# A gated mix of a long convolution and an MLP: sorting the filter with GpSimd before its transposes

## The chip, the cores and the metric

The kernel runs on one core of one Trainium2 chip. The metric is the time of one launch on the device in microseconds (us); lower is better. The engines are named as in the profile: PE is TensorE (PEld its weight loads), DVE is VectorE, ACT is ScalarE, POOL is GpSimd, and SP is SyncE, which here only issues transfers.

## The reference

Two branches read the same input `x = A_q` (2048 rows of 640) and are mixed by one gate per row. Cut to what matters:

```python
x = A_q
g = sigmoid((x * gate_w).sum(-1, keepdims=True))

# branch A: a short filter on k (4 taps), times v, then a long filter over the rows, per column
k_shift = sum(k_pad[:, t:t + S, :] * shift_k[:, ks - 1 - t] for t in range(4))
kv = k_shift * v
y = irfft(rfft(pad(kv)) * rfft(pad(ssm_k)))[:S] + kv * ssm_D
a = q * y

# branch B: an MLP over shifted groups of columns, and a second MLP
h = gelu(layernorm(x) @ w1)
x1 = x + shifted(h) @ w2
b = x1 + gelu(layernorm(x1) @ w3) @ w4

out = g * a + (1 - g) * b
```

`A_ssm_k`, the long filter, is given with columns along the first axis: 640 by 2048. The convolution needs it as rows by columns, like `kv`.

## The kernel before

The 2048 rows lie on 128 partitions with 16 rows each (`NT = 16`); the 640 columns are five chunks of 128 (`DC = 5`). The convolution is a Fourier transform made of matrix products with tables of sines: `step1` transforms the rows of `KV` (the product of the short filter and v) and of `HT0` (the long filter), writes the result to a scratch tensor in memory (`S_x`, `S_h`), `gather` reads it back in another order, `step2` makes the second stage, `product` multiplies the two spectra, `step3`, `S_g`, `gin` and `step4` go back. Beside it run `mlp1`, `w2` (first MLP) and `w3`, `w4` (second MLP).

Nothing is scheduled by the compiler: the text `ORDER` is one long list of steps, such as `step1.KV.3.VAVAVAAAAA:2` (second part of a call with its arguments), and `emit` runs through it. Each engine executes its own instructions in that order. Letters in a name say which engine empties a PSUM tile: `A` for ACT, `V` for DVE (`evac`, L323 to L327). A planner wrote the list; only the list is in the kernel.

What the change touches:

- `load_h` brings one chunk of the long filter (128 columns by 2048 rows, 512 KB) into SBUF. Chunks 0 to 2 share a large tile `E`; chunks 3 and 4 take a buffer `HN` of a ring of four (tag `gt`). The same ring later holds index tables (`n`, `ab`), a row of gate sums (`zr`), a tile of ones and the MLP's `gt` tiles. Whoever takes a buffer of the ring waits until its former owner has been read.
- `h_transpose` (L340 to L358) turns a chunk for `HT0`. Partition p of the wanted layout holds even rows in its lower half and odd rows in its upper half, so each step of 16 is turned by two transposes of 64 columns of weights each, one for each half of the array (L352): 32 per chunk, 160 in all. ACT or DVE then empties PSUM into `HT0`.
- `kv_consts` (L500) makes `DG`, 20 diagonal matrices of the short filter's taps, by one DVE multiplication of the identity with the taps (L503). `tap` (L543) uses them: it multiplies transposed chunks of k (`KT`) with these diagonals on PE, and DVE multiplies with v in place (L554 or L557).
- `x_stats`, `rstd_of` (L610, L611), `x_norm` (L617), `x_turn`: statistics of four rows of x, their reciprocal roots on POOL, the normed rows `xn`, and their transposition, for groups 0 and 1 on PE and for 2 and 3 by a transposing DMA (L605).
- `z_rows` (L674 on PE, four ACT copies to `zr` at L679, four small DMAs to `Zs` at L682) and `z_cols` make the sums for the gate.
- `v_load` issues an indirect DMA on POOL's queue (L150) behind whatever POOL was given before.
- `h_shift` copies shifted parts of the MLP's hidden layer into `HM` on DVE (L719, L700, L703).

The half transposes and the rule of the ring, as the code has them:

```python
for r in range(2):
    PE.transpose(out=ps[HALF[r], i, :], in_=hv[:, 8 * hh + i, r, :], identity=IDB[:], tile_position=(0, H * r))
hn = ring.tile([P, S], BF16, name="HN", tag="gt", bufs=GTB)
```

Of the kernel before, what the change touches and what calls it, by code (L numbers as in the profile page):

```python
# [10 lines left out]
ALU = mybir.AluOpType  # L11
BF16 = mybir.dt.bfloat16
# [4 lines left out]
P = 128  # L17
# [3 lines left out]
NT = 16  # L21
H = 64
NG = 32
DC = 5
# [17 lines left out]
def kernel(  # L42
# [23 lines left out]
    GTB = 4  # L66
# [272 lines left out]

    def h_transpose(dc, ev):  # L340
        if "HT0" not in st:
            st["HT0"] = main.tile([P, NT * D], BF16, name="HT0", tag="RT")
        hv = st.pop(("HN", dc)).rearrange("p (t2 r t1) -> p t1 r t2", r=2, t1=NT)
        dst = st["HT0"][:].rearrange("p (t d) -> p t d", t=NT)
        def make(hh):
            box = {}

            def first():
                ps = box["ps"] = psc.tile([P, 8, P], BF16, name="pst", tag="c")
                for i in range(8):  # L350
                    for r in range(2):
                        PE.transpose(out=ps[HALF[r], i, :], in_=hv[:, 8 * hh + i, r, :], identity=IDB[:], tile_position=(0, H * r))  # L352

            def second():
                evac(ev[hh], dst[:, 8 * hh:8 * hh + 8, dc * P:(dc + 1) * P], box["ps"][:])
            return first, second

        return banks(2, make)  # L358
# [141 lines left out]
    def kv_consts():  # L500

        st["DG"] = pool("A2").tile([P, DC * 4, P], BF16, name="DG")
        V.tensor_tensor(out=st["DG"][:], in0=IDB[:].unsqueeze(1).to_broadcast([P, DC * 4, P]),  # L503
                        in1=st["cr"][:].rearrange("p k j -> p (k j)").unsqueeze(2).to_broadcast([P, DC * 4, P]), op=ALU.mult)
# [310 lines left out]
    def step4(t1, ev):  # L815
# [32 lines left out]
        "open.L1.left:0 open.A2.right:0 kv_alloc:0 warm:0 load_x0.0:0 consts0:0 load_x0.1:0 k_load.3.AAA:0 load_cj:0 "  # L848
        "consts0:1 f4_table:0 f1_table:0 k_load.1.AAV:0 k_load.2.AAA:0 f4_table:1 f1_table:1 load_x.1:0 k_load.0.AAA:0 "
        "x_stats.0.VVVA:0 x_stats.0.VVVA:1 x_stats.0.VVVA:2 x_stats.0.VVVA:3 x_stats.0.VVVA:4 row_order:0 load_w1:0 "  # L850
        "k_load.3.AAA:5 load_gw:0 k_load.3.AAA:6 k_load.3.AAA:3 k_load.3.AAA:1 k_load.1.AAV:1 k_load.1.AAV:5 "
        "x_stats.0.VVVA:5 k_load.3.AAA:4 k_load.1.AAV:3 load_x.3:0 k_load.3.AAA:2 k_load.1.AAV:2 kv_consts:0 "
        "k_load.2.AAA:3 v_load.3:0 k_load.1.AAV:4 x_stats.0.VVVA:6 x_norm.0.VVVV:0 x_norm.0.VVVV:1 x_norm.0.VVVV:2 "
        "k_load.1.AAV:6 k_load.2.AAA:1 k_load.2.AAA:4 k_load.2.AAA:2 d_fold:0 x_turn.0.VAV:0 x_norm.0.VVVV:3 "
        "x_turn.0.VAV:4 v_load.2:0 k_load.2.AAA:5 x_turn.0.VAV:1 x_turn.0.VAV:2 k_load.2.AAA:6 x_turn.0.VAV:3 "
        "x_turn.0.VAV:5 tap.7.AA:0 tap.7.AA:1 k_load.0.AAA:1 k_wrap:0 tap.9.VA:0 x_stats.1.VVVV:0 x_stats.1.VVVV:1 "
        "x_stats.1.VVVV:2 x_stats.1.VVVV:3 tap.9.VA:1 tap.7.AA:3 k_load.0.AAA:2 load_h.0:0 tap.7.AA:4 x_stats.1.VVVV:4 "
        "k_load.0.AAA:5 tap.9.VA:3 mlp1.0.1:0 tap.5.AV:0 v_load.1:0 x_stats.1.VVVV:5 tap.9.VA:2 k_load.0.AAA:6 "
        "load_x.2:0 tap.7.AA:2 tap.5.AV:3 tap.5.AV:4 mlp1.0.1:1 w1_mixed:0 tap.5.AV:1 tap.6.VA:0 tap.6.VA:1 tap.6.VA:2 "
        "tap.8.VA:0 k_load.0.AAA:3 tap.5.AV:2 mlp1.0.0:0 load_h.1:0 x_norm.1.VVVV:0 x_norm.1.VVVV:1 x_norm.1.VVVV:2 "  # L860
        "x_norm.1.VVVV:3 x_stats.3.VVAA:0 x_stats.3.VVAA:1 tap.6.VA:3 v_load.0:0 tap.8.VA:1 x_stats.3.VVAA:2 "
        "x_turn.1.AAV:4 tap.8.VA:3 x_stats.3.VVAA:3 k_load.0.AAA:4 x_turn.1.AAV:2 x_turn.1.AAV:5 x_turn.1.AAV:0 "
        "x_stats.3.VVAA:4 mlp1.0.2:0 x_stats.3.VVAA:5 x_stats.3.VVAA:6 tap.8.VA:4 x_stats.3.VVAA:7 x_turn.1.AAV:3 "
        "tap.8.VA:2 tap.4.AV:0 tap.6.VA:4 x_turn.1.AAV:1 mlp1.0.0:1 tap.4.AV:1 tap.9.VA:4 x_norm.3.VVVV:0 tap.4.AV:3 "
        "x_norm.3.VVVV:1 tap.4.AV:4 x_norm.3.VVVV:2 tap.3.AA:0 mlp1.0.2:1 x_norm.3.VVVV:3 tap.3.AA:1 mlp1.1.1:0 "
        "tap.3.AA:3 step1.KV.3.VAVAVAAAAA:0 x_stats.2.VVAA:0 step1.KV.3.VAVAVAAAAA:1 step1.KV.3.VAVAVAAAAA:6 "
        "x_stats.2.VVAA:1 x_stats.2.VVAA:2 x_stats.2.VVAA:3 step1.KV.3.VAVAVAAAAA:2 step1.KV.3.VAVAVAAAAA:7 mlp1.1.0:0 "
        "tap.3.AA:4 step1.KV.3.VAVAVAAAAA:8 x_stats.2.VVAA:4 x_stats.2.VVAA:5 tap.0.VV:0 x_stats.2.VVAA:6 x_turn.3.D:0 "
        "tap.4.AV:2 tap.0.VV:3 tap.0.VV:1 mlp1.1.0:1 load_h.3:0 tap.2.AA:0 mlp1.1.1:1 x_stats.2.VVAA:7 tap.0.VV:4 "
        "mlp1.1.2:0 tap.0.VV:2 x_norm.2.VVVA:0 tap.2.AA:3 step1.KV.3.VAVAVAAAAA:3 x_norm.2.VVVA:1 x_norm.2.VVVA:2 "  # L870
        "tap.2.AA:1 step1.KV.3.VAVAVAAAAA:4 x_norm.2.VVVA:3 h_shift.0:0 step1.KV.3.VAVAVAAAAA:5 "
        "step1.KV.3.VAVAVAAAAA:9 step1.KV.3.VAVAVAAAAA:11 mlp1.1.2:1 mlp1.3.0:0 t2_table:0 step1.KV.3.VAVAVAAAAA:10 "
        "tap.2.AA:4 step1.KV.3.VAVAVAAAAA:12 step1.KV.3.VAVAVAAAAA:13 h_shift.0:1 mlp1.3.0:1 tap.1.VV:0 mlp1.3.2:0 "
        "tap.1.VV:1 h_shift.0:2 x_turn.2.D:0 step1.KV.3.VAVAVAAAAA:14 tap.2.AA:2 step1.KV.3.VAVAVAAAAA:16 mlp1.3.1:0 "
        "step1.KV.2.VAAVVAAVAV:6 tap.1.VV:3 tap.1.VV:2 mlp1.3.2:1 step1.KV.2.VAAVVAAVAV:8 tap.1.VV:4 "
        "step1.KV.3.VAVAVAAAAA:15 tap.3.AA:2 step1.KV.2.VAAVVAAVAV:3 step1.KV.2.VAAVVAAVAV:4 t2_table:1 mlp1.2.1:0 "
        "step1.KV.2.VAAVVAAVAV:5 step1.KV.2.VAAVVAAVAV:7 step1.KV.1.AVVAVVAAVA:9 mlp1.3.1:1 step1.KV.1.AVVAVVAAVA:11 "
        "h_shift.1:0 step1.KV.1.AVVAVVAAVA:6 h_shift.0:3 step1.KV.1.AVVAVVAAVA:8 mlp1.2.2:0 step1.KV.1.AVVAVVAAVA:10 "
        "mlp1.2.1:1 load_w2:0 step1.KV.1.AVVAVVAAVA:0 step1.KV.1.AVVAVVAAVA:1 load_h.2:0 h_shift.3:0 h_shift.3:1 "
        "step1.KV.1.AVVAVVAAVA:7 z_rows:0 h_shift.1:1 step1.KV.1.AVVAVVAAVA:12 step1.KV.1.AVVAVVAAVA:2 mlp1.2.0:0 "  # L880
        "mlp1.2.2:1 z_rows:1 step1.KV.1.AVVAVVAAVA:14 step1.KV.1.AVVAVVAAVA:13 step1.KV.1.AVVAVVAAVA:3 "
        "step1.KV.1.AVVAVVAAVA:5 h_shift.3:2 z_rows:2 h_shift.2:0 step1.KV.2.VAAVVAAVAV:9 h_shift.1:2 "
        "step1.KV.1.AVVAVVAAVA:4 step1.KV.2.VAAVVAAVAV:10 w2.0:0 h_shift.2:1 step1.KV.2.VAAVVAAVAV:11 "
        "step1.KV.2.VAAVVAAVAV:0 w2.0:1 mlp1.2.0:1 step1.KV.2.VAAVVAAVAV:12 step1.KV.2.VAAVVAAVAV:13 "
        "step1.KV.2.VAAVVAAVAV:1 h_shift.2:2 w2.15:0 h_transpose.0.VV:2 h_shift.1:3 h_transpose.2.AV:2 "
        "step1.KV.2.VAAVVAAVAV:2 t2_table:2 h_transpose.1.VA:2 step1.KV.2.VAAVVAAVAV:14 h_transpose.0.VV:3 "
        "h_transpose.2.AV:3 w2.15:1 h_transpose.1.VA:0 h_transpose.2.AV:0 h_transpose.2.AV:1 h_transpose.1.VA:1 "
        "h_transpose.0.VV:0 w2.2:0 step1.KV.0.AAAAVAAAAA:0 step1.KV.1.AVVAVVAAVA:16 h_transpose.1.VA:3 "
        "step1.KV.1.AVVAVVAAVA:15 h_transpose.0.VV:1 step1.KV.0.AAAAVAAAAA:1 step1.KV.0.AAAAVAAAAA:6 h_shift.3:3 "
        "load_h.4:0 step1.KV.0.AAAAVAAAAA:8 w2.2:1 step1.KV.0.AAAAVAAAAA:7 step1.KV.0.AAAAVAAAAA:2 w2.12:0 "  # L890
        "step1.KV.0.AAAAVAAAAA:12 w2.2:2 step1.KV.2.VAAVVAAVAV:15 step1.KV.0.AAAAVAAAAA:9 step1.KV.0.AAAAVAAAAA:10 "
        "t2_table:3 t2_table:4 step1.KV.0.AAAAVAAAAA:11 w2.1:0 w2.12:1 step1.KV.0.AAAAVAAAAA:13 "
        "step1.KV.0.AAAAVAAAAA:14 step1.KV.0.AAAAVAAAAA:3 h_shift.2:3 step1.KV.0.AAAAVAAAAA:5 step1.KV.2.VAAVVAAVAV:16 "
        "step1.KV.0.AAAAVAAAAA:4 h_transpose.4.AV:0 h_transpose.4.AV:2 h_transpose.4.AV:3 h_transpose.3.AV:0 "
        "h_transpose.4.AV:1 h_transpose.3.AV:2 z_cols:0 load_w3:0 w2.1:1 h_transpose.3.AV:3 h_transpose.3.AV:1 "
        "step1.KV.0.AAAAVAAAAA:16 step1.KV.0.AAAAVAAAAA:15 z_cols:1 w2.0:2 z_cols:2 w2.3:0 i_tables:0 "
        "step1.HT0.2.AAVAAAAVAA:6 step1.HT0.2.AAVAAAAVAA:8 step1.HT0.2.AAVAAAAVAA:3 step1.HT0.2.AAVAAAAVAA:5 "
        "step1.HT0.2.AAVAAAAVAA:4 z_cols:3 w2.3:1 step1.HT0.2.AAVAAAAVAA:7 w2.10:0 w2.10:1 w2.1:2 swap.A2.C.right:0 "
# [156 lines left out]
```

## Time and profile before

| what | value |
|---|---|
| median of 3 runs | 241.06 us (240.78 to 244.64) |
| the profiled execution | 242.35 us, of which the span of instructions is 240.6 us |
| mean granted clock of PE in it | 0.984 |
| busy: PE, DVE, ACT, POOL | 227.9, 193.3, 170.4, 19.1 us |
| transposes of the long filter (L352) | 160 matmuls, 5.6 us (from `E`) and 3.8 us (from `HN`) of PE busy time |
| the diagonals (L503, DVE) | 1 instruction, 2.83 us, begun at 8.73 us |
| bytes moved by DMA | 57.08 MB, mean 237 GB/s |

The page of a profile gives each engine's busy time, then the span in 40 slices of 6 us with a digit for tenths of busy time, then the chain of work that ended last: for each instruction what released it, back to the start. A group of instructions is a line of code, an engine, an operation and shapes, with its count, its total busy time and the mean of one in ns. Matmuls overlap each other on PE, so the mean of one is longer than the step from one to the next; the step is read from the chain. Times inside the span are counted from its start.

### The profile page before, as it was taken

The page shows a single profiled execution, that of the slowest core. Times are in us where ns is not written, and L with a number is a line of the kernel's source. Part 1 is how long each engine was busy: PE and PEld are TensorE (multiplying, and loading weights), DVE is VectorE, ACT ScalarE, POOL GpSimd, SP SyncE. Part 2 cuts the span into 40 slices and gives each one's busy share as a digit, 9 for nine tenths or more (in the row PEclk, how much of TensorE's full clock was granted, in tenths as well). Part 3 has the DMA queues.
Part 4 walks back from the last instruction along what each step waited for, and adds up shares of the span by engine and source line. Part 5 has one row for each costly group of instructions (what it writes and reads, how often), then busy time and mean ns, then how long its engine had stood idle before and what let it go on. Part 6 is the DMA issues. An engine that isn't in the chain of part 4 may idle for free.

```text
span 240.6 us, 5764 instructions
## 1 busy us (share of the span) xinstructions
PE 227.9 (95%) x2328; PEld 117.7 (49%) x2328; DVE 193.3 (80%) x449; ACT 170.4 (71%) x303; POOL 19.1 (8%) x32
## 2 busy tenths in 40 slices
PE   6598999999999999999999999999999999989991
PEld 2585755433858445344355334444444345446660
DVE  7876999988876999756679999867688999209994
ACT  4689999779587899899577677675598533436530
POOL 3540322000000020002200300000000000000000
PEclk9689999999999999999999999999999999999999
DMA  6999608693989889994989936199830127689674
GB/s 218 389 379 417 224 2 198 163 343 121 348 302 344 207 346 277 374 385 170 291 206 271 207 121 223 34 244 392 318 110 3 48 107 259 214 301 347 147 276 165
DMA packets 42744, 57.08 MB, mean 237 GB/s; under 512 B 20313, under 2 KB 35418, under 8 KB 42462
## 3 DMA queue, kind: packets, MB, share of 16 engines
q1 hardware_dynamic: 42142, 54.10, 68.5%
q0 software_dynamic: 576, 2.62, 2.9%
q8 instruction: 18, 0.29, 0.5%
q14 instruction: 8, 0.07, 0.1%
HBM read 34.42 MB, written 18.36 MB: 219 GB/s over the span
## 4 chain that ended last, share of the span: by engine, by line
PE 74%; DMA 13%; DVE 9%; POOL 2%; issue 1%; SPq 0%; DVEq 0%
PE ps L788 20%; PE ps L806 15%; PE psw L740 10%; PE psm L663 8%; PE ps L378 5%; PE ps L417 4%; DMA KV<-in_A_v_dram,ROWS 4%; PE pst L352 4%; PE ps L464 3%; PE psk L543 3%; DMA ax<-S_h 2%; DMA q<-in_A_q_dram 2%; DMA gin<-S_g 2%; DVE X L843 2%; DVE q L839 2%; POOL RS L610 2%
## 5 line engine op out<-in xcount | busy, mean ns | idle before, releaser
L806 PE MATMUL ps<-W,gt 128*128 128x512 bf16 (+1 forms) x384 | 56.6, 300 | 0.0
L788 PE MATMUL ps<-x1t,W 128*128 128x512 bf16 x240 | 55.6, 380 | 0.0
L806 PEld LDWEIGHTS <-gt 128*128 128x128 bf16 x384 | 29.0, 98 | 24.9 <-issue 4.6
L788 PEld LDWEIGHTS <-W 128*128 128x128 bf16 x240 | 21.8, 98 | 29.2 <-issue 5.6
L325 ACT CAST stg<-ps 128x512 bf16<-128x512 f32 x51 | 27.3, 597 | 6.7 <-PE ps L378 5.8
L793 ACT ACTIVATE gt<-ps 128x1024 bf16<-128x1024 f32 x24 | 24.8, 1031 | 6.4 <-PE ps L788 6.1
L325 ACT CAST gs<-ps 128x320 bf16<-128x320 f32 x36 | 13.9, 431 | 16.7 <-PE ps L464 11.7
L663 PE MATMUL psm<-xt,WA 128*128 128x512 bf16 x100 | 23.5, 380 | 0.0
L740 PE MATMUL psw<-WA,HT 128*128 128x512 bf16 (+1 forms) x116 | 21.5, 300 | 0.0
L327 DVE CAST stg<-ps 128x512 bf16<-128x512 f32 x29 | 19.3, 683 | 2.5 <-PE ps L378 1.9
L325 ACT CAST hs<-ps 128x512 bf16<-128x512 f32 x28 | 15.2, 591 | 8.3 <-PE ps L417 8.2
L327 DVE CAST gs<-ps 128x320 bf16<-128x320 f32 x28 | 12.7, 485 | 5.6 <-PE ps L464 3.8
L833 ACT ACTIVATE y<-ps,GS 128x320 bf16<-128x320 f32 x19 | 9.7, 526 | 10.0 <-PE ps L829 8.5
L327 DVE CAST XS<-ps 128x512 bf16<-128x512 f32 x18 | 11.8, 684 | 5.7 <-PE ps L417 5.7
L808 DVE SCALAR_TENSOR_TENSOR X<-ps,OMG,X 128x640 bf16<-128x640 f32 x16 | 14.0, 877 | 1.7 <-PE ps L806 1.7
L839 DVE SCALAR_TENSOR_TENSOR q<-ps,GS,q 128x320 bf16<-128x320 f32 x13 | 7.1, 546 | 9.7 <-PE ps L829 9.7
L325 ACT CAST XS<-ps 128x512 bf16<-128x512 f32 x22 | 11.9, 593 | 4.0 <-PE ps L417 3.7
L740 PEld LDWEIGHTS <-HT 128*128 128x128 bf16 x116 | 9.3, 98 | 11.2 <-issue 3.0
L663 PEld LDWEIGHTS <-WA 128*128 128x128 bf16 x100 | 9.0, 98 | 11.5 <-issue 1.6
L742 DVE SCALAR_TENSOR_TENSOR X<-psw,X 128x640 bf16<-128x640 f32 x16 | 12.9, 818 | 0.9 <-PE psw L740 0.7
L417 PE MATMUL ps<-ax,CMP 64*32 64x512 bf16 (+3 forms) x512 | 13.0, 300 | 0.5 <-DMA ax<-S_h 0.5
L745 ACT ACTIVATE jk<-X 128x640 bf16<-128x640 bf16 x16 | 12.0, 751 | 0.0
(141 smaller groups left out, 356.0 us busy)
## 6 DMA issues: line engine op xcount, KB each, us to landing
S_x<-stg SPq DMA_DIRECT2D x8, 640.0 KB
ax<-S_x SPq DMA_DIRECT2D x8, 640.0 KB
S_h<-stg SPq DMA_DIRECT2D x8, 640.0 KB
ax<-S_h SPq DMA_DIRECT2D x8, 640.0 KB
S_g<-gs SPq DMA_DIRECT2D x8, 640.0 KB
W<-in_B_w_dram SPq DMA_DIRECT2D x2, 1920.0 KB
kn<-in_A_k_dram SPq DMA_DIRECT2D x4, 640.0 KB
q<-in_A_q_dram SPq DMA_DIRECT2D x4, 640.0 KB
```

What stands on the lines that cost most here:

```text
L325: A.copy(out=dst, in_=src)
L327: V.tensor_copy(out=dst, in_=src)
L378: PE.matmul(ps[r][:], lhsT=F1[HALF[r]].rearrange("p a b -> p (a b)"), rhs=src[HALF[r], o + 512 * u:o + 512 * u + 512], start=True, stop=Tr ...
L417: PE.matmul(ps[j][q:q + 32, lo - 512 * u:hi - 512 * u], lhsT=CMP[HALF[j], 8 * b + 4 * h + i, c, :], rhs=st[name, 2 * b + h][HALF[j], i, lo ...
L663: PE.matmul(ps[:, v, :].rearrange("p (a b) -> p a b", a=4), lhsT=W1N[:, k, 160 * f:160 * f + P] if f < 4 else W1M[:, k, :], rhs=xt[:, :, k ...
L740: PE.matmul(ps[:, o:o + w], lhsT=h_tile(f, t1), rhs=W2P[:, f, o:o + w], start=(f == 0), stop=(f == 4))
L742: V.scalar_tensor_tensor(out=X1[:, t1, :], in0=ps[:], scalar=1.0, in1=X[:, t1, :], op0=ALU.mult, op1=ALU.add, accum_out=S12[:, 0, t1:t1 + 1])
L745: A.activation(out=jk[:], in_=X1[:, t1, :], func=ACT.Square, accum_out=S12[:, 1, t1:t1 + 1])
L788: PE.matmul(ps[:, u, :].rearrange("p (a b) -> p a b", a=4), lhsT=st["W3"][:, k, f * P:(f + 1) * P], rhs=xt[:, :, k, :], start=(k == 0), st ...
L793: A.activation(out=gt[:, 2 * (fp % 2):2 * (fp % 2) + 2, :], in_=ps[:], func=ACT.Gelu_apprx_tanh)
L806: PE.matmul(ps[:, o:o + w], lhsT=st["gt", c, f // 4][:, f % 4, i * P:(i + 1) * P], rhs=st["W4"][:, f, o:o + w], start=(f == 0), stop=(f == ...
L808: V.scalar_tensor_tensor(out=X1[:, t1, :], in0=ps[:], scalar=OMG[:, t1:t1 + 1], in1=X1[:, t1, :], op0=ALU.mult, op1=ALU.add)
```

## The change

Three things change, and with them the whole list.

1. A new step `h_sort` lets POOL copy each loaded chunk of the filter into a new tile `HP` (a buffer of the ring `gt`), sorted so that the 64 even and 64 odd rows of a step lie behind one another. It reads every 32nd element of two bytes and writes densely. `h_transpose` then turns 128 by 128 elements at once: 16 per chunk, 80 in all.
2. `DG` is made by one POOL select from the taps, spread over the diagonal, instead of DVE's multiplication.
3. `ORDER` is written anew (the letters too), with five `h_sort` steps in it.

```diff
+    def h_sort(dc):
+        hp = ring.tile([P, NT, 2, H], BF16, name="HP", tag="gt", bufs=GTB)
+        G.tensor_copy(out=hp[:], in_=st.pop(("HN", dc)).rearrange("p (q r t) -> p t r q", r=2, t=NT))
+        st["HP", dc] = hp[:].rearrange("p t r q -> p t (r q)")
+
     def h_transpose(dc, ev):
...
-        hv = st.pop(("HN", dc)).rearrange("p (t2 r t1) -> p t1 r t2", r=2, t1=NT)
+        hv = st.pop(("HP", dc))
...
-                    for r in range(2):
-                        PE.transpose(out=ps[HALF[r], i, :], in_=hv[:, 8 * hh + i, r, :], identity=IDB[:], tile_position=(0, H * r))
+                    PE.transpose(out=ps[:, i, :], in_=hv[:, 8 * hh + i, :], identity=IDB[:])
...
-        V.tensor_tensor(out=st["DG"][:], in0=IDB[:].unsqueeze(1).to_broadcast([P, DC * 4, P]),
-                        in1=st["cr"][:].rearrange("p k j -> p (k j)").unsqueeze(2).to_broadcast([P, DC * 4, P]), op=ALU.mult)
+        G.affine_select(out=st["DG"][:], in_=st["cr"][:].rearrange("p k j -> p (k j)").unsqueeze(2).to_broadcast([P, DC * 4, P]), compare_op=ALU.is_equal, fill=0.0,
+                        base=0, pattern=[[0, DC * 4], [-1, P]], channel_multiplier=1)
```

Of the new list, the part that the prediction speaks of most, around the five sorts (cut):

```diff
+        "... step1.KV.3.VAAVAAVAAA:4 tap.0.AV:3 tap.0.AV:1 tap.0.AV:4 h_sort.4:0 x_turn.2.D:0 tap.4.AV:0 tap.4.AV:3 "
+        "tap.4.AV:4 h_sort.3:0 step1.KV.3.VAAVAAVAAA:15 ... tap.0.AV:2 z_rows:0 step1.KV.2.AAVAVAAAAV:4 "
+        "step1.KV.3.VAAVAAVAAA:16 mlp1.3.2:1 tap.1.VA:3 z_rows:1 ... z_rows:2 ... "
+        "step1.KV.1.VAAVVAVAVA:6 h_sort.1:0 ... h_transpose.3.AA:0 h_shift.1:2 h_transpose.4.VV:0 ... "
+        "h_transpose.1.VA:2 ... h_transpose.1.VA:0 ... h_sort.2:0 w2.3:0 ... w2.15:0 ... h_sort.0:0 ... w2.2:0 ... "
+        "h_transpose.2.AV:2 ... h_transpose.2.AV:0 h_transpose.2.AV:1 h_transpose.0.VV:0 ..."
```

On POOL's own queue the order becomes: the constants, the ones of `z_cols`, the row numbers, two v loads (chunks 3 and 2), the roots of `x_stats.0`, the select for `DG`, the v load of chunk 0, the roots of `x_stats.1`, the v load of chunk 1, the roots of `x_stats.3` and of `x_stats.2`, the five sorts (chunks 4, 3, 1, 2, 0), then the four roots of `x1_norm`. Before, the first v load stood ahead of the first roots and the next two behind them. The waits that the new list gives to the sorts: the sort of chunk 4 waits for its load and for an early table on ACT; that of chunk 3 for its load and for the sort of chunk 4; that of chunk 1 for the four small DMAs of `z_rows` (its buffer held `zr`); that of chunk 2 for the last transpose of chunk 1; that of chunk 0 for the last transpose of chunk 4. The copies to `zr` on ACT wait for the sort of chunk 3.

## The prediction

> **What bounds the kernel now.** I read the page's busy times and slices first.
>
> ```profile
> PE 227.9 (95%) x2328; PEld 117.7 (49%) x2328; DVE 193.3 (80%) x449; ACT 170.4 (71%) x303; POOL 19.1 (8%) x32
> PE   6598999999999999999999999999999999989991
> DVE  7876999988876999756679999867688999209994
> POOL 3540322000000020002200300000000000000000
> ```
>
> PE is full from the fourth slice to the tail; POOL all but idle after the seventh. Whether full means bound is read in the chain that ended last, in order of time (start, length, what):
>
> ```profile
> 12.90 10.10 DMA KV<-in_A_v_dram,ROWS
> 23.13 0.42 DVE KV L554
> 23.70 0.60 DVE KV L557
> 24.35 1.99 PE psk L543 x38
> ...
> 61.66 5.50 PE pst L352 x96
> ...
> 72.95 3.71 PE pst L352 x64
> ...
> 206.84 3.40 DMA S_g<-gs
> 210.26 5.35 DMA gin<-S_g
> ```
>
> From 24.35 to 205.9 us nearly every piece is PE: a us less of PE work there is a us less of time, as long as nobody keeps PE waiting. DVE has little to spare beside it: by windows of 6 us it is idle only 0.24, 0.63, 0.64, 0.81, 1.70 and 1.99 us between 42 and 78 us, 6.0 in all. Then the groups of single instructions, for the prices:
>
> ```profile
> L571 PE MATMUL pst<-IDB,xn 128*128 128x128 bf16 x40 | 2.9, 219 | 0.3 <-ACT KT L325 0.3
> L352 PE MATMUL pst<-IDB,E 128*64 128x128 bf16 x96 | 5.6, 276 | 0.0
> L352 PE MATMUL pst<-IDB,HN 128*64 128x128 bf16 x64 | 3.8, 276 | 0.0
> L209 POOL TENSOR_SCALAR_AFFINE_SELECT IDB<-IDB 128x128 bf16<-128x128 bf16 x1 | 0.3, 292 | 0.1
> ```
>
> Last, POOL and DVE side by side in the timeline:
>
> ```profile
> 8.73 2.83 DVE L503 TENSOR_TENSOR DG<-IDB,cr 128x2560 bf16<-128x2560 bf16 x1
> 8.76 3.71 POOL L610 TENSOR_TENSOR RS<-VE,EXPO 128x4 f32<-128x4 f32 x1 [5.29 <-DVE VE L648]
> 23.79 1.05 POOL L610 TENSOR_TENSOR RS<-VE,EXPO 128x4 f32<-128x4 f32 x1 [8.62 <-DVE VE L648]
> 24.21 0.41 DVE L554 TENSOR_TENSOR KV<-yk,KV 128x512 bf16<-128x512 bf16 x1
> ```
>
> The same root of 128x4 took 3.71 us when DVE's multiplication of two SBUF tensors ran over it and 1.05 us otherwise; 2.65 us is almost that multiplication's length. So POOL stands while DVE reads two SBUF tensors.
>
> **Transposes.** 160 half ones take 5.50 + 3.71 = 9.21 us of the chain, 57 ns each. Whole ones of `xn` stand in the chain as 20 in 1.12 us (56 ns), those of `kn` as 8 in 0.55 (69 ns). 80 cost 4.5 to 5.5 us; `HP` is dense like `xn`, so 4.5: -4.7 us (-3.7 to -4.7).
>
> **The end.** Before, two first loads of `gin` queue behind the last `S_g` store, and PE stands 0.76 us for them. In the new order three steps of `w3` and one of `w4` still lie between the last `step3` and the first `step4`, with one such load behind the store: -0.8 us. The tail after it has the same PE work and one `step4` half fewer on DVE: 0.
>
> **The start.** The first two v loads now pass POOL's roots, so the 1.22 us that PE stands before 24.35 can go; next late are k and w1, since the DMA share is 0.99 to 1.02 from 6 to 24 us. Against it, the select for `DG` stands on POOL between the first roots and `v_load.0`, and the four `xn` of group 0 meet it on DVE. Its price: 20 of the 0.292 us select, 5.8 us, at most; at least 2560 by the slope between iotas of 7 and 64 elements (0.148 and 0.200 us), 2.3 us. DVE saves the 2.83. I take 0 in sum, -1.2 to +3.
>
> **One sort.** Nothing on POOL of this size is in the trace. From below the iota slope gives 2048 x 0.91 ns = 1.9 us, from above 16 of the 128-element select 4.7 us. Reading every 32nd element is unlike a dense sweep, so I take the upper end, 4.7. The Trainium skill ("GPSIMD Engine Reference", performance pitfalls) gives 2.9 cycles an element instead of 1.9 where the read steps over 8 bytes; at its 1.2 GHz an estimate is 4.95 us a sort, and the sums below would grow by about 1 us. No row here shows it.
>
> **What a sort holds up.** The rows show DVE holding POOL, not the reverse. I assume that it holds in both directions, for copies SBUF to SBUF too: DVE's `xn` and `h_shift` wait for a running sort, and all behind them on DVE. The Trainium skill ("SBUF — State Buffer", who interferes with whom) says so: the one that starts first has the shared ports for its whole instruction. The row at 24.21 speaks against "whole": that product reads two SBUF tensors in 0.41 us, its usual time, inside the root that began at 23.79; but a root of 4 elements needs the ports briefly.
>
> Three places follow, each at 4.7 us:
> - A, `xn` of group 2. Its roots ended at 40.96 us before, and little in front has changed. The sort of chunk 4 follows at once on POOL, loaded long before, to 45.7. DVE then does one `xn`; the sort of chunk 3 takes its turn, to 50.8; the other `xn` end at 51.7. The transposing DMA takes 2.47 us to issue and an estimated 1.5 to land (under 4.4 by the first reader before): 55.7. Its next reader, `z_rows`, stood at 53.54 and has 4.4 us less PE work ahead: due at 49.2. PE waits 6.5 us; 1.7 if all `xn` slip between the sorts, 0 if DVE isn't held.
> - B, the sort of chunk 1. It waits for `zr`'s DMAs. Behind `z_rows`: four ACT copies of 0.576, the last issue 0.25, landing about 2 (between 1 and the 3.4 of `S_g`), ACT's queue 0.6, the sort: 9.9 us. PE has 8.2 us of work until the chunk's transposes (2 x 2.27 and 1.13 of `mlp1`, six `step1` of 0.27, two half chunks of transposes at 0.46): +1.7 us; nothing below a sort of 3.0.
> - C, the sort of chunk 0 runs behind that of chunk 2, which waits for chunk 1's transposes: 9.4 us against 7.6 of PE work (three `w2` of 1.47, five `step1`, four half chunks): +1.8 us; nothing below 3.8.
> - The last three sorts also meet `h_shift`. With 4.5 us of DVE idle from 60 to 78, I put +2 (0 to 6).
>
> Sum: -4.7 - 0.8 + 0 + 6.5 + 1.7 + 1.8 + 2.0 = +6.5 us. The profiled execution has 1.75 us around its span; 242.35 + 6.5 = 248.9. It lies 1.3 us over the median; the same against 241.06 is 247.5.
>
> **Rivals.**
> - The gain arrives, the other sign: a sort takes 3 us or less, or holds DVE no more than the root held the product at 24.21. A, B and C are hidden, the start gives 0 to 1.2: 241.06 - 5.5 = 235.6, 234.4 at best. For it: POOL has almost nothing to do from 42 to 86 us, and these loads are early. It decides below 3.0 us a sort.
> - Half of it: the sort takes 4.7 but DVE isn't held. B and C alone, 3.5 us: 239.1; with A at 1.7 or a slow start up to 245. For it: the row at 24.21; against it: 8.76.
> - Worse: DVE can do only about 1 us of other work under each sort and loses 5 x 3.7 = 18.5 us, of which its 6.0 us of idle time take up a part: 12.5 late, and `step1` and `w2`, which need its evacuations, with it. With C 241.06 - 5.5 + 12.5 + 1.8 = 250, to 254. Against it: half of DVE's work after 57 us empties PSUM, which nothing here shows to meet POOL.
> - That the transposes don't get cheaper: at 69 ns the gain is still 3.7, inside these widths.
>
> **The numbers.** Sum as forecast 0.36 (245 to 251), worse 0.12 (249 to 254), gain arrives 0.30 (233.5 to 236.6), half 0.22 (237 to 245). The likeliest gives 247.5, its own range 245 to 251. Cases of both signs hold the chance, so the range runs from 234.5 to 251.5; it leaves out a third of the gain's and half of the worse case's chance, 0.16. 2%, about what a measurement of this kernel can tell from no change, is 236.2 and 245.9: faster 0.28 (all of the gain but 0.02), slower 0.46 (the worse case and 0.34 of the forecast's), within 0.26.
>
> **What would show it.** The duration of the five copies on POOL: under 3 us is the first rival. An `xn` or a copy to `HM` far over its 0.44 and 0.28 us, or idle time before it that ends with POOL, shows that DVE is held. Idle PE before `z_rows` confirms A, before chunk 1's transposes B, before chunk 0's C. Transposes of `HP` at about 56 ns in the chain confirm the gain. The step I trust least is the length of a sort; next, that DVE is held at all. The forecast also falls if stalls lie outside 40 to 70 us, where the new order itself would be the cause.

## The result, and the profile after

| | us |
|---|---|
| before, median of 4 runs beside it | 242.12 |
| after, median of 4 runs | 259.45 (257.70 to 260.18) |
| ratio | 1.0725, 95% interval 1.062 to 1.083 |
| the profiled execution after | 260.18, span 258.3, mean granted clock of PE 0.949 |

The change costs 17.3 us; 247.5 was forecast and 251.5 was the upper end. The busy times and slices of the page, with the granted clock:

```profile
PE 230.7 (89%) x2232; PEld 118.3 (46%) x2248; DVE 207.2 (80%) x448; ACT 169.8 (66%) x305; POOL 36.9 (14%) x38
PE   7369999469794899999999999999999999999992
POOL 5153026600546000100110000030000000000000
PEclk9956999959979799999999999999999999999998
...
PE 63%; DVE 20%; DMA 10%; issue 3%; ACT 1%; SPq 1%; DVEq 0%; ACTq 0%
```

The first line is busy time, share and count by engine, the next three are slices of 6.46 us, the last is the chain by engine. PE has holes in the second and third slice and from the eighth to the fourteenth, each followed by a lower clock; from the fifteenth on it is as full as before. POOL is at work where the later holes begin, and DVE now holds 20% of the chain, before 9%. The five sorts, and what DVE did beside them, stand in the timeline (start, length, engine, line, operation; in brackets the idle time before and what ended it):

```profile
41.99 7.34 POOL L342 COPY HP<-HN 128x2048 bf16<-128x2048 bf16 x2
65.18 3.64 POOL L342 COPY HP<-E 128x2048 bf16<-128x2048 bf16 x1 [15.84 <-DMA Zs<-zr]
74.64 7.31 POOL L342 COPY HP<-E 128x2048 bf16<-128x2048 bf16 x2 [5.82 <-PE pst L356]
...
43.22 6.65 DVE L621 TENSOR_SCALAR xn<-X,RS,NB 128x640 bf16<-128x640 bf16 x3
...
53.11 1.29 DVE L327 CAST stg<-ps 128x512 bf16<-128x512 f32 x2
65.48 3.72 DVE L723 COPY HM<-HT 32x512 bf16<-32x512 bf16 x2
75.28 3.17 DVE L723 COPY HM<-HT 32x512 bf16<-32x512 bf16 x1
78.48 0.69 DVE L327 COPY HT<-pst 128x1024 bf16<-128x1024 bf16 x1
79.20 3.83 DVE L286 TENSOR_TENSOR n<-ab 128x1024 int32<-128x1024 f32 x1
```

A sort lasts 3.67 us. Three `xn` last 6.65 us instead of 1.16, two copies to `HM` 3.72 instead of 0.58, one 3.17 instead of 0.28, the table's product 3.83 instead of 1.22: each ends behind the end of a sort, by no more than its own usual length. The copy from PSUM at 78.48 takes its usual 0.69 us although a sort runs. What this did to PE is in the same view:

```profile
53.85 0.58 PE L547 MATMUL psk<-DG,KT 64*128 64x256 bf16 x3 [5.52 <-DVE stg L327]
70.66 0.37 PE L382 MATMUL ps<-KV,F 64*128 64x512 bf16 x1 [1.60 <-DVE stg L327]
79.22 0.59 PE L382 MATMUL ps<-KV,F 64*128 64x512 bf16 x3 [1.39 <-DVE HT L327]
84.42 0.39 PE L382 MATMUL ps<-KV,F 64*128 64x512 bf16 x2 [2.82 <-DVE stg L327]
```

None of these waits of PE ends with POOL. They end with DVE's copies out of PSUM (`stg`, `HT`), which are short themselves but stand in DVE's queue behind the held ones: the two `stg` at 53.11 come behind the three `xn` and what was queued after these.

How 240.6 us of span became 258.3 follows from windows of 6 and 12 us over both traces. Idle PE is the window less its busy time; what a low clock costs is the busy time multiplied by the missing share of the clock.

| part of the span after | idle PE, more than before | low clock, more than before |
|---|---|---|
| 0 to 30 us | 2.1 | 1.3 |
| 42 to 60 | 5.5 | 2.1 |
| 60 to 90 | 6.5 | 3.0 |
| 90 to the end | 0.8 | 0 |

From 30 to 42 us PE is full in both. That is 14.9 idle and 6.4 of clock, 21.3 us. PE's busy time grew by 2.8 only, so its work shrank by 6.4 - 2.8 = 3.6 us, which I put down to the whole transposes. 21.3 - 3.6 = 17.7.

### The profile page after: what moved, and what is told of

It reads as the page before. It is cut to its first block, busy times and chain, and to the rows that moved or that the text cites. A ratio compares the mean times of both kernels' runs of the same rounds, so it can differ in the third digit from the quotient of the medians.

```text
span 258.3 us, 5596 instructions
## 1 busy us (share of the span) xinstructions
PE 230.7 (89%) x2232; PEld 118.3 (46%) x2248; DVE 207.2 (80%) x448; ACT 169.8 (66%) x305; POOL 36.9 (14%) x38
## 4 chain that ended last, share of the span: by engine, by line
PE 63%; DVE 20%; DMA 10%; issue 3%; ACT 1%; SPq 1%; DVEq 0%; ACTq 0%
PE ps L792 17%; PE ps L810 14%; PE psw L744 6%; PE psm L667 6%; PE psk L547 5%; DMA kn<-in_A_k_dram 4%; PE ps L421 4%; DVE HM L723 3%; PE pst L575 3%; PE ps L382 3%; DVE xn L621 3%; PE ps L468 2%; PE pst L356 2%; DVE X L847 2%; DMA q<-in_A_q_dram 2%
## 5 line engine op out<-in xcount | busy, mean ns | idle before, releaser
L810 PE MATMUL ps<-W,gt 128*128 128x128 bf16 (+1 forms) x373 | 55.3, 297 | 0.7 <-issue 0.3
L325 ACT CAST stg<-ps 128x512 bf16<-128x512 f32 x55 | 29.6, 604 | 12.7 <-PE ps L382 9.8
L325 ACT CAST gs<-ps 128x320 bf16<-128x320 f32 x45 | 16.3, 437 | 17.1 <-PE ps L468 12.1
L327 DVE CAST stg<-ps 128x512 bf16<-128x512 f32 x25 | 16.6, 686 | 3.2 <-PE ps L382 2.2
L547 PE MATMUL psk<-DG,KT 64*128 64x256 bf16 (+3 forms) x190 | 13.7, 294 | 5.5 <-DVE stg L327 5.5
L325 ACT CAST hs<-ps 128x512 bf16<-128x512 f32 x20 | 10.8, 593 | 10.5 <-PE ps L421 9.8
L327 DVE CAST hs<-ps 128x512 bf16<-128x512 f32 x20 | 13.2, 685 | 5.3 <-PE ps L421 5.2
L614 POOL TENSOR_TENSOR rn<-ve,EXPO 128x4 f32<-128x4 f32 x4 | 4.0, 1008 | 85.2 <-DVE ve L759 85.2
L667 PEld LDWEIGHTS <-WA 128*128 128x128 bf16 x100 | 9.0, 98 | 11.9 <-issue 2.2
L547 PEld LDWEIGHTS <-KT 64*128 64x128 bf16 x190 | 10.5, 114 | 8.2 <-issue 6.9
L342 POOL COPY HP<-E 128x2048 bf16<-128x2048 bf16 x3 | 11.0, 3670 | 21.7 <-DMA Zs<-zr 15.8
```

What stands on the lines that cost most here:

```text
L325: A.copy(out=dst, in_=src)
L327: V.tensor_copy(out=dst, in_=src)
L342: G.tensor_copy(out=hp[:], in_=st.pop(("HN", dc)).rearrange("p (q r t) -> p t r q", r=2, t=NT))
L547: PE.matmul(ps[e][:, lo:hi, :], lhsT=kt[a], rhs=st["DG"][a, 4 * k + lo - i:4 * k + hi - i, a], start=(i == 0), stop=(i == 7))
L667: PE.matmul(ps[:, v, :].rearrange("p (a b) -> p a b", a=4), lhsT=W1N[:, k, 160 * f:160 * f + P] if f < 4 else W1M[:, k, :], rhs=xt[:, :, k ...
L810: PE.matmul(ps[:, o:o + w], lhsT=st["gt", c, f // 4][:, f % 4, i * P:(i + 1) * P], rhs=st["W4"][:, f, o:o + w], start=(f == 0), stop=(f == ...
```

## The experiments

The rivals, as they stood before the first run: H, a running sort holds DVE's copies within SBUF, and DVE's queue then starves PE; O, the new order stalls by itself; C, the waits and the lateness of the sorts, as the forecast's B and C had them.

**No sorts, in the new order.** `h_sort` does nothing, `h_transpose` is that of before:

```diff
     def h_sort(dc):
-        hp = ring.tile([P, NT, 2, H], BF16, name="HP", tag="gt", bufs=GTB)
-        G.tensor_copy(out=hp[:], in_=st.pop(("HN", dc)).rearrange("p (q r t) -> p t r q", r=2, t=NT))
-        st["HP", dc] = hp[:].rearrange("p t r q -> p t (r q)")
+        return
```

> The changed kernel with its order and its select for DG, but h_sort does nothing and h_transpose turns the loaded chunk by 160 half transposes as before; everything is computed. Theory H (a running sort holds DVE's copies, DVE then empties PSUM late, PE stands and its clock falls): the 12.0 us of idle PE and the 5 us lost to a low clock between 48 and 90 us go, 4.6 us of PE work come back: 260.2 - 17 + 4.6 = 247 to 249 us. Theory O (the new order of the steps itself stalls): the stalls stay, 260 to 265. Theory C (only the sorts' own waits and lateness, forecast as B and C): the stall at 48 to 54 us stays, those from 66 to 90 go (idle 6.4, clock about 3): 253 to 256.

Measured 246.9 us, 1.019 (1.013 to 1.025) of the kernel before. The stall at 48 us is gone, PE is full from 24 to 84 us. The new order with its select costs some 4.7 us; the other 12.5 belong to the sorts, less what the whole transposes give back.

**Sorts that nobody reads.** As the kernel without sorts, plus:

```diff
     def h_sort(dc):
+        hp = st["E"][:, 3 * S:3 * S + 12 * P].rearrange("p (t r q) -> p t r q", t=12, r=2)
+        G.tensor_copy(out=hp, in_=st["HN", dc].rearrange("p (q r t) -> p t r q", r=2, t=NT)[:, 0:12])
```

> As the kernel without sorts (160 half transposes from the loaded chunks), but GpSimd still makes five strided copies at the same steps, of 12 of the 16 steps of each chunk into an unused part of E; nobody reads them, so no transpose waits for one. They wait for their loads alone. Theory H: 5 copies of 3.67 x 12/16 = 2.75 us hold DVE 13.8 us; with about 1 us of DVE work fitting under each, 8 to 11 us over the kernel without sorts, with xn or copies to HM that last as long as the copy they meet. Theories O and C: within 1 us of the kernel without sorts.

Measured 258.8 us, 1.068 (1.057 to 1.079). The timeline:

```profile
41.33 5.62 POOL L342 COPY E<-HN 128x1536 bf16<-128x1536 bf16 x2
47.01 5.55 POOL L342 COPY E<-E 128x1536 bf16<-128x1536 bf16 x2
...
42.56 7.38 DVE L621 TENSOR_SCALAR xn<-X,RS,NB 128x640 bf16<-128x640 bf16 x3
49.87 3.20 DVE L723 COPY HM<-HT 32x512 bf16<-32x512 bf16 x2
...
56.49 0.58 PE L547 MATMUL psk<-DG,KT 64*128 64x256 bf16 x3 [8.82 <-DVE stg L327]
```

13.9 us of GpSimd copies on which nothing depends cost 258.8 - 246.9 = 11.9 us. This is the test that shows H: no step waits for these copies, and PE's stall ends with DVE's copy out of PSUM. The first four, here back to back, cost PE one stall of 8.82 us. O and C forecast no change.

**Sorts of chunks 1, 2 and 0 without their waits.** They write into `KT` instead of a ring buffer:

```diff
-        hp = ring.tile([P, NT, 2, H], BF16, name="HP", tag="gt", bufs=GTB)
+        if dc in (3, 4):
+            hp = ring.tile([P, NT, 2, H], BF16, name="HP", tag="gt", bufs=GTB)[:]
+        else:
+            hp = flat(st["KT"][:].rearrange("p a b c -> p (a b) c"))[:, dc * S:(dc + 1) * S].rearrange("p (t r q) -> p t r q", r=2, t=NT)
```

> The changed kernel, but the sorts of chunks 1, 2 and 0 write into KT, which the short filter has done with, instead of a buffer of the ring: they no longer wait for the DMAs of zr or for other chunks' transposes. Theory H: they come earlier and still hold DVE; the stall at 48 to 54 us stays and the later one moves forward, 254 to 261 us. Theory C: the stalls from 66 to 90 us go: 249 to 252.

Two runs, 255.2 and 259.5 us. They are too far apart for a ratio, but both lie above the 249 to 252 of theory C.

**The same sorts on ACT** (`A.copy` for `G.tensor_copy`):

> As the kernel with KT for chunks 1, 2 and 0, but ACT makes all five sorted copies instead of GpSimd. Theory H: DVE's copies keep their usual 0.28 to 0.44 us; ACT's queue gets some 5 x 2 us more, of which part shows where ACT was full (24 to 48 us): 242 to 250 us. Theories O and C: within 3 us of the kernel with KT.

A miss: 257.8 and 262.0 us. ACT needed as long as GpSimd for this access, which I had put at 2 us without a row for it. The profile is of the longer run. The groups of the two kernels' copies, the first from the change itself, the second from this run (count, busy us, mean ns):

```profile
L342 POOL COPY HP<-E 128x2048 bf16<-128x2048 bf16 x3 | 11.0, 3670 | 21.7 <-DMA Zs<-zr 15.8 <-PE pst L356 5.8
```

```profile
L345 ACT COPY KT<-E 128x2048 bf16<-128x2048 bf16 x3 | 11.0, 3672 | 0.0
```

DVE's product of two SBUF tensors kept its 0.41 us while ACT sorted, but ACT has its own evacuations behind 18.3 us of sorts, and DVE stood 6.28 us for ACT at 59 us. So the run shows a second way to starve PE; it doesn't speak against H.

**The core of the change in the old order.** The kernel before, sorts by GpSimd into `KT` from 45 us on, whole transposes:

```diff
+        G.tensor_copy(out=hp, in_=st.pop(("HN", dc)).rearrange("p (q r t) -> p t r q", r=2, t=NT))
...
-                    for r in range(2):
-                        PE.transpose(out=ps[HALF[r], i, :], in_=hv[:, 8 * hh + i, r, :], identity=IDB[:], tile_position=(0, H * r))
+                    PE.transpose(out=ps[:, i, :], in_=hv[:, 8 * hh + i, :], identity=IDB[:])
```

> The kernel before, with its own order and its own DG, plus five sorts on GpSimd into KT (free once the short filter is done) and 80 whole transposes: the core of the change alone. Theory H: five sorts of 3.67 us hold DVE some 12 us in all, as the unread copies did (258.8 against 246.9 us), 4.6 us of PE work go: 242.2 + 12 - 4.6 = 247 to 252 us. If the new order was what made the hold costly (its sorts meet xn and the copies to HM of the shift), less is lost here: 238 to 244.

Measured 252.6 us, 1.047 (1.043 to 1.052). The loss, 11.4 us, is about that of the sorts in the new order. Its timeline shows which DVE instructions are held:

```profile
45.26 7.26 POOL L342 COPY KT<-E 128x2048 bf16<-128x2048 bf16 x2 [4.25 <-ACT stg L325]
52.46 3.83 POOL L342 COPY KT<-HN 128x2048 bf16<-128x2048 bf16 x1
57.05 4.14 POOL L342 COPY KT<-E 128x2048 bf16<-128x2048 bf16 x1 [0.75 <-DMA E<-in_A_ssm_k_dram]
...
49.09 3.72 DVE L558 TENSOR_TENSOR KV<-yk,KV 128x512 bf16<-128x512 bf16 x1
52.73 1.28 DVE L561 TENSOR_TENSOR KV<-psk,KV 128x512 bf16<-128x512 f32 x2
53.93 2.65 DVE L558 TENSOR_TENSOR KV<-yk,KV 128x512 bf16<-128x512 bf16 x1
56.50 1.21 DVE L286 TENSOR_TENSOR n<-ab 128x1024 int32<-128x1024 f32 x1
57.75 4.00 DVE L240 TENSOR_SCALAR n<-n 128x1024 int32<-128x1024 int32 x1
```

The product of `yk` and `KV`, both in SBUF, waits for the sort's end (2.65 us instead of 0.41). The product of `psk`, in PSUM, with `KV` runs through at its usual 0.64 us a piece, in the midst of the sort that began at 52.46. At 56.50 the table's product was first: it ends at 57.71, and the sort that was to begin at 57.05 takes 4.14 instead of 3.67 us. So whichever starts first is served first, in both directions.

**The sort cut into eight copies of two steps**, in the changed kernel:

```diff
+        for t in range(0, NT, 2):
+            G.tensor_copy(out=hp[:, t:t + 2], in_=hn[:, t:t + 2])
```

> The changed kernel with each sort cut into eight copies of two steps (128x256, about 0.46 us each by 1.79 ns an element). Theory H with the hold lasting one instruction: DVE gets in between two pieces and waits for one at a time, so its copies last up to 0.5 us longer instead of 3.7; the sorts last longer: 249 to 255 us. If GpSimd keeps the access from piece to piece, 257 to 261 us.

Measured 250.9 us, 1.040 (1.037 to 1.044): 8.5 us are won by cutting alone, though the sorts get longer: two chunks take 10.35 us instead of 7.34. A piece lasts 0.69 us on average where 1.79 ns an element would give 0.46. The shortest takes 0.61, so most of the difference is a price that each piece has for itself; waiting for DVE shows in the longest, 1.62 us under the table's product at 72 us. Three `xn` take 1.99 us instead of 6.65. The stall before 54 us is 3.75 instead of 5.52. DVE gets in between two pieces: the hold lasts one instruction.

**Runs of 32 bytes.** The parts of a chunk that must change places are runs of 16 neighbouring elements. A sort can move whole runs, and the weight load then takes every 16th element; the first kernel does so on GpSimd, the second on DVE at other places of the list, both in the old order (the second against the kernel above, cut):

```diff
-        G.tensor_copy(out=hp, in_=st.pop(("HN", dc)).rearrange("p (q r t) -> p t r q", r=2, t=NT))
+        V.tensor_copy(out=hp, in_=st.pop(("HN", dc)).rearrange("p (q r t) -> p r q t", r=2, t=NT))
```

> As the kernel before with sorts on GpSimd, but the sort moves runs of 16 elements (32 bytes) and leaves the step between rows to the weight load (a column every 32 bytes instead of every 64). If the steps of 64 bytes made the copy slow (1.79 ns an element, against 0.91 by the slope between the two iotas of the start), a sort takes 1.9 to 2.2 us and the hold is about half: 240 to 246 us. If GpSimd's copy costs by the element whatever the step, 3.67 us and the same time as with sorts by element.

> As that, with the five copies of runs on DVE, placed where it had idle time (before z_rows up to the w2 steps at 72 us). DVE's 128x512 copies take 0.28 us, so 2048 elements take about 1.1 us, 5.5 in all, against 4.5 us of idle DVE from 60 to 78 us: 238 to 241 us if most of it fits; if the rows of 32 bytes are as slow as on ACT and GpSimd (3.67 us), 250 us and more.

Measured 244.2 us, 1.012 (1.002 to 1.022), and 241.8 us, 1.0004 (0.995 to 1.006). The groups of the sorts, first by GpSimd, then by DVE:

```profile
L342 POOL COPY KT<-E 128x2048 bf16<-128x2048 bf16 x3 | 5.7, 1909 | 10.3 <-DMA E<-in_A_ssm_k_dram 6.1 <-ACT stg L325 4.3
```

```profile
L342 DVE COPY KT<-E 128x2048 bf16<-128x2048 bf16 x3 | 2.1, 691 | 0.1
```

The same 2048 elements take 3.67 us element by element and 1.91 by runs on GpSimd, and 0.69 on DVE, where I had estimated 1.1. With half the hold, the loss against the kernel before falls from 11.4 to 2.9 us; with none it is gone. But nothing is won either, and that was open.

**Where the transposes' gain goes.** One more kernel in the new order and three in the old. The first sorts runs on DVE, those of chunks 1, 2 and 0 into `KT`, with everything else of the change as it is:

> The changed kernel, its order and its select for DG, with the sorts as DVE copies of runs of 32 bytes (0.69 us each; chunks 1, 2 and 0 into KT). Theory H: what is left is the order's own price, the kernel without sorts less the whole transposes' gain: 246.9 - 3.6 + 0 to 2 = 243 to 246 us. If the sorts' places in the list were what cost, 250 and more.

Measured 244.5 us, 1.012 (1.002 to 1.022): 15.0 us less than the change, by its sorts and where they write alone.

The others bound the gain. One has whole transposes and no sort (`rearrange("p (t m) -> p t m", t=NT)` on the loaded chunk, so the filter's rows stand in another order); one has DVE's sorts unread and half transposes:

> The kernel before with 80 whole transposes of 128 neighbouring elements straight from the loaded chunk: no sort anywhere, so the filter's rows stand in another order in HT0 and the output is not the reference's. Everything else is as before. If the transposes' 9.21 us of the chain are worth what the chain says, 80 x 56 ns = 4.5 us take their place: 237 to 238 us against 241.5 to 242.4. If the gain is given back elsewhere (the end waits for gin, DVE and ACT empty the turned chunks no faster), 239.5 to 242.

> The kernel before with the five sorts of runs on DVE, but nobody reads them: 160 half transposes from the loaded chunks. It shows what DVE's 3.45 us more cost: 242 to 244 us if PE waits for DVE as in the kernel that used the sorts (about 1.2 us of stalls before 95 us); then the whole transposes are worth the difference, 2 to 3 us. If DVE's copies cost nothing, the same as before.

Measured 242.4 us, 1.003 (0.999 to 1.007), and 241.8 us, 1.003 (1.000 to 1.006). DVE's 3.45 us of copies cost next to nothing, and 4.6 us less of PE work at no price bring nothing. The windows of both traces show why. Columns: the stretch, its length, then busy time (and instructions) of PE, PE's weight loads, DVE, ACT and POOL, the granted clock, the busy share of the DMA engines, GB/s. Before:

```profile
66.00:70.00 4.00, 4.00 (x41) 2.34 (x39) 2.44 (x6) 2.91 (x5) 0.00 (x0) 1.00 0.79 260
78.00:82.00 4.00, 4.00 (x31) 1.76 (x28) 3.64 (x9) 3.46 (x8) 0.00 (x0) 1.00 0.68 102
82.00:86.00 4.00, 4.00 (x31) 1.77 (x28) 3.84 (x10) 3.73 (x9) 0.00 (x0) 1.00 0.95 354
```

Whole transposes without a sort:

```profile
66.00:70.00 4.00, 4.00 (x47) 2.54 (x45) 3.53 (x8) 4.00 (x10) 0.20 (x1) 1.00 1.03 414
78.00:82.00 4.00, 3.93 (x29) 1.77 (x26) 3.64 (x12) 3.60 (x8) 1.20 (x2) 1.00 1.03 368
82.00:86.00 4.00, 1.96 (x16) 0.86 (x13) 1.93 (x6) 1.92 (x4) 0.00 (x0) 1.00 1.01 416
```

The same kernel's chain, and PE's timeline at the end:

```profile
68.58 1.94 PE pst L351 x32
...
77.89 6.08 DMA S_h<-stg
84.07 1.16 DVE xn L616 x3
85.23 0.75 DVE X L741 x2
86.02 4.55 PE psw L739 x20
```

```profile
214.61 2.88 PE L828 MATMUL ps<-gin,F 128*128 128x320 bf16 x20 [1.99 <-DMA gin<-S_g]
```

After its last transposes PE is 6.1 us ahead of the kernel before (70.53 against 76.66), 1.5 of them from the start. Then the stores to `S_h` go out 6.2 us earlier, with the DMA engines full, and take 6.08 us; `xn` of the next group needs one of their buffers, and PE stands 2.06 us at 86 and loses 1.6 to a clock of 0.61 behind it. At the first `w3` 2.3 us are left (94.40 against 96.72), and at the first `step4` 1.1, because PE now waits 1.99 us for `gin` instead of 0.76. The span ends 1.5 us sooner, as much as the start had given.

**Two attempts at more.** Both sort runs on DVE, with the sort of chunk 4 a step earlier; one moves a `w3` of 2.3 us behind the last `step3`, the other one part of `w4` (1.45 us), to cover the wait for `gin`:

> The kernel before with five sorts of runs on DVE (0.69 us each in the run before) and 80 whole transposes, the sort of chunk 4 one step earlier, and one w3 (2.3 us of PE) moved behind the last step3, where PE stood 1.70 us for gin. Transposes save 80 x (2 x 57 - 69 ns) = 3.6 us, DVE's sorts cost PE about 1 us of stalls, the moved w3 saves up to 1.7: 237 to 240 us against 241 to 242. If DVE's 3.45 us more cannot be hidden before z_rows or the transposes, 241.

> The kernel before with the sorts of runs on DVE and whole transposes, the sort of chunk 4 one step earlier, and instead of the whole w3 only one short part of w4 (1.45 us of PE) moved behind the last step3, where PE stood 1.70 us for gin; the w3 that covered the step3 halves stays in its place, so the 1.4 us of idle PE and the low clock from 186 to 198 us should not come back: 239 to 241 us; if taking any cover from the step3 halves costs as much as it brings, 241 to 243.

Measured 243.9 us, 1.008 (1.004 to 1.012), and 243.7 us, 1.007 (1.004 to 1.011): misses. Whole transposes with DVE's sorts had left 1.70 us of waiting for `gin` before the first `step4`. That wait went in both (the second waits 0.76 us for a later `gin`), but what had been moved was cover: PE stood 1.44 us between two `step3` in the first, at 188 us, and 2.91 us for DVE's and ACT's last evacuations in the second, from 201 to 207.

**Start and select.** The kernel without sorts with the second v load moved back, and the kernel before with the select for `DG` alone:

> The kernel without sorts, with the second v load moved back behind POOL's first roots. If that early load is what delays the third load of k (10.4 us in flight, PE idle 3.0 us for it), PE stands less before 18 us: 244 to 246 us against 246.9. If the k load is late for its own place in the queue (it is issued at 3.1 us behind two more loads than before), nothing changes: 246 to 248.

> The kernel before with DG made by GpSimd's select alone. The select took 2.47 us on GpSimd in the changed kernel, and the roots fall from 3.71 to 1.05 us as DVE's multiplication (2.83 us) is gone; the first v loads of chunks 3 and 2 lie behind them: within 1.5 us of the kernel before, 240.5 to 243.5. If the select holds DVE's xn of group 0 so that PE waits, 243 to 245.

Measured 245.6 us, 1.017 (1.008 to 1.026), against 246.9 for the kernel without sorts; and 241.8 us, 1.001 (0.997 to 1.006). With the v load moved back it is 1.3 us less, but the two intervals overlap, so a price of this load isn't shown. PE still gets the third load of k at 13.84 us only (13.56 without the move), and waits 1.72 us at 22 us for the first MLP's weights, which the kernel before doesn't. The select costs nothing in the old order. Where the new order's own 4.7 us arise stays open for the most part.

## Why the prediction was wrong

- **How a sort reaches PE: the step that failed.** The forecast let the hold act at three places of its own, "A" by `xn`, the transposing DMA and `z_rows`, "B" and "C" by the sorts' chains, with 2.0 us for the rest. In fact whatever DVE has behind a held instruction waits with it, and PE stops at the next full PSUM tile: at 48.3 us for `stg`, not at `z_rows`. For A, 6.5 us were put and 5.5 + 2.1 lost to the clock measured; for B, C and the rest 5.5 were put, and 6.5 + 3.0 measured. These two make 5.1 of the 11.2 us by which the span missed its +6.5; the start makes 3.4, the end 1.6, the transposes 1.1. The unread sorts have neither chain and still cost 11.9 us, so the chains are no needed part. The rival "worse" (0.12) had this mechanism, 250 to 254 us; what I held against it, that evacuations from PSUM don't meet POOL, is true and doesn't help. Even its upper end is 5.4 us short: it had neither the start nor the clock.
- **The assumption that DVE is held both ways** is right. The row at 24.21, my reason for the two cheaper rivals, met a root of four elements; why that root didn't hold DVE no run shows. The Trainium skill ("SBUF — State Buffer", who interferes with whom) names DVE instructions with two SBUF inputs and those in its two-port modes, and says that the first to issue keeps the ports for its whole instruction: the rows at 52.73, 53.93 and 57.05 of the old order's timeline agree.
- **The sort's length**: 3.67 us, not 4.7; both bounds held it. By my rule it should have helped: A would have been 2.1 us smaller, B 1.0 smaller, and C gone. The Trainium skill's 2.9 cycles an element ("GPSIMD Engine Reference", performance pitfalls for Q7 kernels), an estimate of 4.95 us, lies further off.
- **The transposes, -4.7**: the price was about right, 3.6 us of work in PE's busy time, and 48 whole ones of dense rows in 2.68 us (56 ns) in the kernel without a sort; those of `HP` ran at a lower clock, 64 in 5.50 us of the chain, and can't confirm it. But "a us less of PE work there is a us less of time" fell: in the old order it is worth 1.003 (0.999 to 1.007) of the time, since transfers stand close behind PE. Even without any hold, 235.6 us was not to be had.
- **The start, 0 (-1.2 to +3)**: 3.4 us lost, just outside. PE waited 3.32 us for the third load of k, until 14.47 us; before, its last wait for k ended at 10.79. I had named k as next late and given it no price. That the early v load is the cause isn't shown, as this load came no earlier with the v load moved back. PE's clock was 0.63 and 0.51 from 12 to 24 us, before 0.63 and 0.80 from 6 to 18.
- **The end, -0.8**: the wait before the first `step4` did go (0.35 us of waiting for `gin` came later), but behind 90 us PE was idle 0.8 us more in all.
- **The lower clock** was no term of the sum: 6.4 us.

## What to carry to other kernels

Before giving an idle GpSimd work that reads SBUF, look at what DVE does in that stretch: here each such instruction stopped DVE's copies and products within SBUF for its whole length, and with them everything queued behind; short instructions, or a form that DVE itself does in 0.69 us, are far cheaper than one of 3.67. Removing work from an engine that is 95% busy on the chain gains only as much as the next chain allows; a kernel that leaves the work out tells how much. A stall of PE cost more than its length: 14.9 us more of idle time came with 6.4 us lost to a lower clock.

## What the runs showed of the hardware

- The same strided copy (2048 two-byte elements, every 32nd) takes 3.67 us on ACT and on GpSimd alike, 1.79 ns an element. By runs of 32 bytes GpSimd takes 1.91 us and DVE 0.69.
- The wait goes both ways: a GpSimd copy of 3.67 us lasted 4.14 behind a DVE product, and a piece of 256 elements, 0.61 at the shortest, 1.62 under another. Cut into such pieces, a sort costs 5.2 us instead of 3.67 but holds DVE for one piece at a time.
- After 5.52 us of idle PE the granted clock was 0.67 from 54 to 60 us; after 2.82 us it was 0.72 from 84 to 90 us.
